# Transposed attention weights copied slot by slot, opening preparation in both banks of a slot, sums spread one period later

## The chip, the cores and the metric

The kernel runs on one core of a Trainium2 chip, in one launch. The metric is the device time of one execution in microseconds (us). Three timed executions of the kernel before took 701.68, 701.98 and 702.99 us; the median is 701.98 us.

## What is computed

The input is attention data q, k, v (2 batches, 8 heads, 1152 rows, 64 columns) and the weights of a small mixture of four experts. All numbers are fp32.

```
q_pool = q.reshape(B, H, S // 2, 2, D).mean(axis=3)      # 576 pooled rows per head
attn   = softmax(q_pool @ k.T / sqrt(D))                  # 576 x 1152 per head
x      = (attn @ v) laid out as 1152 rows x 512 columns
p      = domain_probs / domain_probs.sum(-1)
out    = sum over 4 experts of p[:, e] * (relu(x @ w1[e]) @ w2[e])
```

## The kernel before, in words

**Two stages.** The first 300 us or so are attention, the rest is the mixture of experts (MoE). Attention works on 8 pairs of heads, one after the other (pair 0 to pair 7). A pair has 9 tiles of 128 rows by 1152 columns, and the loop at the end of the attention stage takes one tile per turn. Such a turn is called a period here: period i (0 to 8) of a pair. In front of the loop stands the opening, which prepares pair 0 and computes the scores of the first two tiles.

**A period** issues, in this order: the transposes of tile g (`T_chunk`, twice), the exponentials of tile g+1 (`exps`, ACT), a part of the product with v (`PV_part`, PE), now and then a spread of the sums (`spread_sums`), one piece of preparation for the next pair (`prep_q` or `prep_k`), and the scores of tile g+2 (`scores`). Every engine runs its own instructions strictly in the order in which they are issued here; semaphores tie the engines together. No scheduler moves anything.

**Names in the rows.** `pt` are the transposes of the exponentials on PE: 18 of them, 10 in the first chunk and 8 in the second. `po` is the product with v on PE, with 256 columns (periods 4 to 8) or 320 columns (periods 0 to 3). `spt` is the score product on PE. `sx` on DVE (L254) scales the scores and takes their row minimum, and `sx` on ACT (L260) is the exponential. `aT` is the copy of transposed weights from PSUM. `pq` and `pk` are the transposes that prepare q and k of the next pair. Prepared values are kept as a high and a low part: ACT writes the high part, DVE subtracts it and writes the low part. `pr` is the spread of the reciprocal sums over the partitions (PE, of a diagonal matrix `dg` that POOL builds), `rb` its copy on ACT.

**PSUM.** The transposes, the preparation and the spreads share a pool `ps_t` of two slots. A slot has two banks of 512 words per partition. `T_chunk` fills both banks of a slot, one bank for each half `a` of the rows; everything else uses bank 0 only. The scores have one slot of three banks, so the scores of a tile start only when DVE has read those of the tile before. The pool hands out whichever slot is due by its own rule when the program is built, and it orders accesses: an instruction that touches a slot waits for those before it that touched the same tile, and a new tile in a slot waits for the last reader of the old one.

**The copies.** Each chunk of `T_chunk` has two copies, `for a in range(2)` at L275: half 0 by ACT (L285), half 1 by DVE (L283).

**The spread.** `diag_sums` builds `dg` on POOL at the end of periods 3 and 8; `SPREAD = {7: (0, 0), 0: (-1, 1)}` (L380) calls `spread_sums` in period 7 for the pair itself and in period 0 for the pair before. `finish` uses the result in periods 8 and 3.

Of the kernel before, what the change touches and what calls it, by code (L numbers as in the profile page):

```python
# [8 lines left out]
F32 = mybir.dt.float32  # L9
F32R = mybir.dt.float32r  # L10
AF = mybir.ActivationFunctionType
# [6 lines left out]
def attention_moe_kernel(ctx, tc, q, k, v, probs, w1, w2, out):  # L18
    nc = tc.nc
# [3 lines left out]
    P = 128  # L23
    HALF = 64
# [87 lines left out]
    with ExitStack() as actx:  # L112
        ap = actx.enter_context(tc.tile_pool(name="ap", bufs=1))
        ps_t = actx.enter_context(tc.tile_pool(name="ps_t", bufs=2, space=PSUM))
# [8 lines left out]
        aT = [ap.tile([P, 2, KT, w], F32, name=f"aT{i}") for i, w in enumerate(GW)]  # L123
# [28 lines left out]
        def add_q0(eng, t0, t1):  # L152
            eng.tensor_tensor(
                qs[:, t0:t1], qn[:, t0:t1, 0, :].unsqueeze(2).to_broadcast([P, t1 - t0, 2, D]),
                qn[:, t0:t1, 1, :].unsqueeze(2).to_broadcast([P, t1 - t0, 2, D]), ALU.add)
# [11 lines left out]
        def split_k0(h, t0, t1):  # L167
            hi, lo = khl[:, h, t0:t1, 0, :], khl[:, h, t0:t1, 1, :]
            nc.scalar.activation(hi, kn[:, h, t0:t1], AF.Copy)
            nc.vector.tensor_tensor(lo, kn[:, h, t0:t1], hi.bitcast(F32), ALU.subtract)  # L170
# [9 lines left out]
        def q_split(hi, lo, src):  # L180
            nc.scalar.activation(hi, src, AF.Copy)  # L181
            nc.vector.tensor_tensor(lo, src, hi.bitcast(F32), ALU.subtract)  # L182

        def prep_q(n, c):
            pt = ps_t.tile([P, 2, 512], F32, tag="t", name="pq")[:, 0].rearrange("p (a b) -> p a b", a=4)
            if c == 2:
                src = qs[:, 8].rearrange("p z d -> p (z d)") if n == 0 else qsum[:, 8:].rearrange("p t d -> p (t d)")
                nc.tensor.transpose(pt[:, 0, :], src, ident)
                d, rows = q2m[n % 2], [slice(0, HALF), slice(HALF, P)]
                for r in rows:  # L190
                    nc.scalar.activation(d[r, 0, r], pt[r, 0, r], AF.Copy)
                for r in rows:
                    nc.vector.tensor_tensor(d[r, 1, r], pt[r, 0, r], d[r, 0, r].bitcast(F32), ALU.subtract)
                return
            for i in range(4):
                src = qs[:, 4 * c + i].rearrange("p z d -> p (z d)") if n == 0 else (
                    qsum[:, 2 * i:2 * i + 2].rearrange("p t d -> p (t d)"))
                nc.tensor.transpose(pt[:, i, :], src, ident)
            src = pt.rearrange("p t (s x) -> p s t x", s=2)
            if n == 0:  # L200
                d = [q2[0][:, z, :, 256 * c:256 * c + 256].rearrange("p s (t x) -> p s t x", x=HALF) for z in range(2)]
                q_split(d[0], d[1], src)
                return
            q_split(stq[:, 0], stq[:, 1], src)
            for y in range(2):
                for half in range(2):
                    r = slice(half * HALF, (half + 1) * HALF)
                    dst = q2[n % 2].rearrange("p z s (y x) -> p (z s) y x", y=2)[r, :, y, :]
                    src = stq.rearrange("p z s j x -> p (z s) (j x)")[y * HALF:(y + 1) * HALF]
                    nc.sync.dma_start(dst.bitcast(F32), src.bitcast(F32))  # L210
# [6 lines left out]
        KCH = [(0, 4), (4, 8), (8, 12), (12, 16), (16, 18)]  # L217
        KCH0 = [(0, 4), (4, 8), (8, 9), (9, 13), (13, 17), (17, 18)]

        def prep_k(n, c):  # L220
            f0, f1 = KCH[c] if n else KCH0[c]
            pt = ps_t.tile([P, 2, 512], F32R, tag="t", name="pk")[:, 0].rearrange("p (a b) -> p a b", a=4)
            for i in range(f0, f1):
                nc.tensor.transpose(  # L224
                    pt[:, i - f0, :], khl[:, i // KT, i % KT].rearrange("p z d -> p (z d)"), identr)
            dst = k2[n % 2].rearrange("p h s -> p (h s)")[:, f0 * P:f1 * P]
            src = pt[:, :f1 - f0, :].bitcast(F32).rearrange("p a b -> p (a b)")
            if c in (1, 3):
                nc.vector.tensor_copy(dst, src)
            else:  # L230
                nc.scalar.activation(dst, src, AF.Copy)
# [26 lines left out]
        def exps(g):  # L258
            n, i = tiles[g]
            nc.scalar.activation(sx[g % 3], sx[g % 3], AF.Exp, bias=mn[g % 3], scale=-1.0,  # L260
                                 accum_out=sums[n % 2][:, i:i + 1])
# [4 lines left out]
        def T_chunk(g, c):  # L266
            n, i = tiles[g]
            k0, k1 = TCH[c]
            ks = slice(k0, k1)
            pt = ps_t.tile([P, 2, 512], F32, tag="t", name="pt")[:, :, :(k1 - k0) * HALF]  # L270
            pt = pt.rearrange("p a (k x) -> p a k x", x=HALF)
            for kt in range(k0, k1):
                for a, r in enumerate(ROWS):
                    nc.tensor.transpose(pt[:, a, kt - k0, :], sx[g % 3][r, kt * P:(kt + 1) * P], ident[r, r])  # L274
            for a in range(2):  # L275
                if i == 8:
                    dst = aT[1][:, a, ks, 256:320]
                else:
                    j, h = divmod(i, 2)
                    x0 = (j % 2) * P + a * HALF  # L280
                    dst = aT[j // 2][:, h, ks, x0:x0 + HALF]
                if a:
                    nc.vector.tensor_copy(dst, pt[:, a])  # L283
                else:
                    nc.scalar.activation(dst, pt[:, a], AF.Copy)  # L285

        opt = {}

# [28 lines left out]
        def spread_sums(n, grp):  # L317
            pt = ps_t.tile([P, 2, 512], F32, tag="t", name="pr")[:, 0]
            w = GW[grp]
            for h in range(2):  # L320
                nc.tensor.matmul(pt[h * HALF:(h + 1) * HALF, :w], ones, dg[:, h, :w], start=True, stop=True)  # L321
            nc.scalar.activation(rb[grp], pt[:, :w], AF.Copy)
# [17 lines left out]
        def scores(g):  # L340
            if g < NTL:
                for c in range(3):
                    S_chunk(g, c)
                neg_scores(g)
# [9 lines left out]
        add_q0(nc.vector, 0, 4)  # L354
        split_k0(0, 0, 4)
        split_k0(0, 4, 9)
        prep_q(0, 0)
        for c in range(3):
            prep_k(0, c)
        add_q0(nc.gpsimd, 4, 9)  # L360
        split_k0(1, 0, 9)
        scores(0)
        for c in range(3, 6):
            prep_k(0, c)
        exps(0)
        scores(1)
        prep_q(0, 1)
        prep_q(0, 2)
        load_q(1)
        load_kv(kn, k, 1)  # L370
# [6 lines left out]
        PVCUT = {0: (1, -1, 0, 3), 1: (1, -1, 3, 5), 2: (1, -1, 5, 7), 3: (1, -1, 7, 9),  # L377
                 4: (0, 0, 0, 2), 5: (0, 0, 2, 4), 6: (0, 0, 4, 6), 7: (0, 0, 6, 8), 8: (0, 0, 8, 9)}
        STAGES = {0: [(stack_k, 0, 0)], 1: [(stack_k, 0, 1)], 3: [(diag_sums, 0, 0)], 8: [(diag_sums, 0, 1)]}
        SPREAD = {7: (0, 0), 0: (-1, 1)}  # L380
        PREP = [None, ("q", 0), ("k", 0), ("k", 1), ("k", 2), ("q", 2), ("k", 3), ("k", 4), None]

        def pv_part(g):
            n, i = divmod(g, 9)
            grp, dn, k0, k1 = PVCUT[i]
            if 0 <= n + dn < NP:
                PV_part(n + dn, grp, k0, k1)
# [28 lines left out]
        for g in range(NTL):  # L416
            n, i = divmod(g, 9)
# [9 lines left out]
            for c in range(2):  # L427
                T_chunk(g, c)
            if g + 1 < NTL:
                exps(g + 1)  # L430
            pv_part(g)
            if i in SPREAD and n + SPREAD[i][0] >= 0:
                spread_sums(n + SPREAD[i][0], SPREAD[i][1])
            if n + 1 < NP:
                if PREP[i]:
                    kind, c = PREP[i]
                    (prep_q if kind == "q" else prep_k)(n + 1, c)
            elif i >= 7:
                fill(4)
# [117 lines left out]
```

## Time and profile before

| what | value |
|---|---|
| median of three timed runs | 701.98 us |
| profiled execution, its own time | 703.03 us |
| span of the profiled execution | 701.2 us |
| busy share: PE, weight loads, DVE, ACT, POOL | 95%, 79%, 38%, 33%, 29% |
| chain that ended last: PE, DVE, issue, POOL, ACT | 80%, 14%, 2%, 2%, 2% |
| attention loop, first to last tile | 16.6 to about 291 us |

The chain that ended last is followed back from the last instruction, at each step to what released it. In the MoE stage it stays on PE. In the attention stage it goes back and forth between PE and DVE, with POOL once per pair. Busy shares are means over two stages with different limits, so they say little about either; a pair of the attention stage is read from the timeline instead. A row of the timeline gives the start, the duration, engine and line, operation and names, and in brackets how long the engine was idle before it and what ended that.

### The profile page before, as it was taken

How to read it: one execution, taken by the hardware profiler on the slowest of the kernel's cores; microseconds unless marked ns; L12 is line 12 of the kernel's file. 1: busy time of each engine (PE TensorE's matmuls, PEld its weight loads, DVE VectorE, ACT ScalarE, POOL GpSimd, SP SyncE). 2: the span in 40 equal slices, each digit the busy share in tenths (PEclk: the TensorE clock that was granted, in tenths of full speed). 3: DMA queues.
4: the chain of work that ended last, by engine and by line, in shares of the span. 5: the costliest groups of instructions: out<-in, count | busy, mean ns of one | idle time of the engine just before them, and what ended most of it. 6: DMA issues, size and time to landing. Idle time of an engine off the chain costs nothing.

```text
span 701.2 us, 11265 instructions
## 1 busy us (share of the span) xinstructions
PE 667.6 (95%) x4634; PEld 551.5 (79%) x4634; DVE 267.4 (38%) x525; ACT 228.9 (33%) x474; POOL 201.5 (29%) x242
## 2 busy tenths in 40 slices
PE   7799999999898989899999999999999999999998
PEld 5666666666666666679898989999898989898987
DVE  5666666666666666422121212122122212121211
ACT  4666666666666666412020101011110101010200
POOL 4213232323232442467061052080080350120000
PEclk7999999999999999999999999999999999999999
DMA  6715353535353770114011011030020010001012
GB/s 221 179 36 125 105 129 104 128 103 131 100 125 106 168 207 3 62 42 139 1 61 60 1 55 65 1 100 20 1 91 31 17 44 1 0 1 31 15 37 56
DMA packets 26452, 50.84 MB, mean 73 GB/s; under 512 B 2464, under 2 KB 9888, under 8 KB 26400
## 3 DMA queue, kind: packets, MB, share of 16 engines
q1 hardware_dynamic: 26400, 50.12, 25.5%
q8 instruction: 37, 0.61, 0.3%
q14 instruction: 15, 0.12, 0.1%
HBM read 30.97 MB, written 2.36 MB: 48 GB/s over the span
## 4 chain that ended last, share of the span: by engine, by line
PE 80%; DVE 14%; issue 2%; POOL 2%; ACT 2%; ACTq 0%; POOLq 0%
PE p L505 28%; PE p L92 27%; PE spt L251 12%; DVE sx L254 10%; PE po L298 4%; PE pk L224 3%; PE pt L274 2%; PE p1t L92 2%; DVE aT L283 2%; PE pr L321 2%; POOL dg L310 1%; DVE q2all L182 1%; POOL dg L314 1%; ACT q2all L181 1%; PE warm L353 0%
## 5 line engine op out<-in xcount | busy, mean ns | idle before, releaser
L92 PE MATMUL p<-xh,wslot 128*128 128x384 f32 x640 | 166.8, 339 | 1.2 <-DVE q2all L95 1.2
L254 DVE TENSOR_SCALAR_CACHE_REDUCE sx<-spt 128x1152 f32<-128x1152 f32 x72 | 97.7, 1356 | 78.0 <-PE spt L251 77.8
L92 PEld LDWEIGHTS p<-xh,wslot 128*128 128x128 f32 x640 | 116.6, 188 | 1.9 <-DVE q2all L95 1.5
L92 PE MATMUL p<-xl,wslot 128*128 128x384 f32 x320 | 108.3, 338 | 0.0
L260 ACT ACTIVATE sx<-sx,mn 128x1152 f32<-128x1152 f32 x72 | 90.6, 1258 | 21.0 <-DVE sx L254 17.9
L251 PE MATMUL spt<-k,q2all 128*128 128x384 f32 x384 | 85.3, 357 | 1.5 <-DVE sx L254 1.2
L298 PE MATMUL po<-aT,vn 128*64 128x320 f32 (+1 forms) x576 | 85.0, 418 | 0.0
L94 ACT ACTIVATE hb<-p 128x384 fp32r<-128x384 f32 x48 | 23.6, 492 | 161.4 <-PE p L92 158.3
L505 PE MATMUL p<-wslot,hb 128*128 128x512 f32 (+1 forms) x348 | 75.8, 375 | 0.0
L285 ACT ACTIVATE aT<-pt 128x320 f32<-128x320 f32 (+1 forms) x144 | 53.0, 409 | 66.7 <-PE pt L274 65.1
L251 PEld LDWEIGHTS spt<-k,q2all 128*128 128x128 f32 x384 | 65.8, 193 | 10.8 <-DVE sx L254 4.8
L505 PEld LDWEIGHTS p<-wslot,hb 128*128 128x128 f32 x348 | 62.2, 188 | 11.7
L510 DVE SCALAR_TENSOR_TENSOR acc<-p,pw,acc 128x512 f32<-128x512 f32 (+1 forms) x28 | 20.5, 731 | 124.1 <-PE p L505 124.1
L274 PEld LDWEIGHTS pt<-ident,sx 64*128 64x128 f32 x1296 | 47.7, 140 | 24.7 <-issue 9.3
L274 PE MATMUL pt<-ident,sx 64*128 64x64 f32 x1296 | 59.4, 230 | 4.0 <-DVE q2all L182 1.2
L92 PEld LDWEIGHTS p<-xl,wslot 128*128 128x128 f32 x320 | 60.0, 188 | 0.4
L283 DVE COPY aT<-pt 128x320 f32<-128x320 f32 (+1 forms) x144 | 58.5, 447 | 1.6 <-ACT aT L285 1.6
L94 ACT ACTIVATE k<-p 128x384 fp32r<-128x384 f32 x30 | 14.8, 492 | 130.6 <-PE p L92 130.6
L338 POOL TENSOR_TENSOR xl<-xs,xh 128x256 fp32r<-128x256 f32 (+2 forms) x20 | 13.4, 677 | 150.9 <-ACT xh L337 150.9
L95 DVE SCALAR_TENSOR_TENSOR hb<-p,hb 128x384 fp32r<-128x384 f32 x48 | 26.8, 558 | 78.1 <-ACT hb L94 78.1
L98 POOL TENSOR_SCALAR wslot<-stg 128x512 fp32r<-128x512 f32 x12 | 7.5, 622 | 161.5 <-PE p L92 84.0
L505 PE MATMUL p<-wslot,k 128*128 128x512 f32 x168 | 51.9, 390 | 0.0
(103 smaller groups left out, 767.1 us busy)
## 6 DMA issues: line engine op xcount, KB each, us to landing
kab<-k SPq DMA_DIRECT2D x32, 288.0 KB, 4.2
q2all<-q2all SPq DMA_DIRECT2D x28, 256.0 KB, 4.9
vn<-in_v_dram SPq DMA_DIRECT2D x8, 576.0 KB, 7.5
kn<-in_moe_w_dram SPq DMA_DIRECT2D x8, 512.0 KB, 3.8
qn<-in_moe_w_dram SPq DMA_DIRECT2D x8, 512.0 KB, 3.8
stg<-in_moe_w_dram SPq DMA_DIRECT2D x8, 512.0 KB, 3.6
qs<-in_moe_w_dram SPq DMA_DIRECT2D x8, 512.0 KB, 3.8
qn<-in_q_dram SPq DMA_DIRECT2D x7, 576.0 KB, 6.5
```

What stands on the lines that cost most here:

```text
L92: nc.tensor.matmul(pt, w[:, a, kt, fs], x[:, kt, cols], start=(j == 0), stop=(j == last))
L94: nc.scalar.activation(hh[ft], pt, AF.Relu)
L95: nc.vector.scalar_tensor_tensor(hl[ft], pt, 0.0, hh[ft].bitcast(F32), ALU.max, ALU.subtract)
L224: nc.tensor.transpose(pt[:, i - f0, :], khl[:, i // KT, i % KT].rearrange("p z d -> p (z d)"), identr)
L251: nc.tensor.matmul(spt[g][:, c, :NC], w, x, start=(j == 0), stop=(j == len(ops) - 1))
L254: nc.vector.tensor_scalar(sx[g % 3].rearrange("p (c x) -> p c x", c=3), spt.pop(g)[:, :, :NC], -INV, None, ALU.mult, ALU.min, accum_out=mn ...
L260: nc.scalar.activation(sx[g % 3], sx[g % 3], AF.Exp, bias=mn[g % 3], scale=-1.0, accum_out=sums[n % 2][:, i:i + 1])
L274: nc.tensor.transpose(pt[:, a, kt - k0, :], sx[g % 3][r, kt * P:(kt + 1) * P], ident[r, r])
L283: nc.vector.tensor_copy(dst, pt[:, a])
L285: nc.scalar.activation(dst, pt[:, a], AF.Copy)
L298: nc.tensor.matmul(po[h * HALF:(h + 1) * HALF, :w], vn[n % 2][:, h, kt, :], aT[grp][:, h, kt, :], start=(kt == 0), stop=(kt == KT - 1))
L505: nc.tensor.matmul(pc, h[ft][:, ts_], where[e, 2, ft // 4][:, a, ft % 4, c0:c1], start=(m == 0), stop=(m == len(ops) - 1))
```

## The change

It has three parts.

**Copies.** `T_chunk` now copies a whole chunk with one instruction: both halves of chunk 0 by ACT, both halves of chunk 1 by DVE.

**Opening.** `prep_q` and `prep_k` may be given a bank. `prep_bank` takes a slot and hands out its two banks one after the other, as parts of one tile; the first eight preparations of the opening use it.

**Spread.** The second spread of a pair moves from period 0 to period 1 of the next pair.

```diff
--- before.py
+++ after.py
@@ -181,8 +181,18 @@
             nc.scalar.activation(hi, src, AF.Copy)
             nc.vector.tensor_tensor(lo, src, hi.bitcast(F32), ALU.subtract)
 
-        def prep_q(n, c):
-            pt = ps_t.tile([P, 2, 512], F32, tag="t", name="pq")[:, 0].rearrange("p (a b) -> p a b", a=4)
+        banks = []
+
+        def prep_bank(name):
+            if not banks:
+                t = ps_t.tile([P, 2, 512], F32, tag="t", name=name)
+                banks.extend([t[:, 0], t[:, 1]])
+            return banks.pop(0)
+
+        def prep_q(n, c, pt=None):
+            if pt is None:
+                pt = ps_t.tile([P, 2, 512], F32, tag="t", name="pq")[:, 0]
+            pt = pt.rearrange("p (a b) -> p a b", a=4)
             if c == 2:
                 src = qs[:, 8].rearrange("p z d -> p (z d)") if n == 0 else qsum[:, 8:].rearrange("p t d -> p (t d)")
                 nc.tensor.transpose(pt[:, 0, :], src, ident)
@@ -217,9 +227,11 @@
         KCH = [(0, 4), (4, 8), (8, 12), (12, 16), (16, 18)]
         KCH0 = [(0, 4), (4, 8), (8, 9), (9, 13), (13, 17), (17, 18)]
 
-        def prep_k(n, c):
+        def prep_k(n, c, pt=None):
             f0, f1 = KCH[c] if n else KCH0[c]
-            pt = ps_t.tile([P, 2, 512], F32R, tag="t", name="pk")[:, 0].rearrange("p (a b) -> p a b", a=4)
+            if pt is None:
+                pt = ps_t.tile([P, 2, 512], F32, tag="t", name="pk")[:, 0]
+            pt = pt.bitcast(F32R).rearrange("p (a b) -> p a b", a=4)
             for i in range(f0, f1):
                 nc.tensor.transpose(
                     pt[:, i - f0, :], khl[:, i // KT, i % KT].rearrange("p z d -> p (z d)"), identr)
@@ -272,17 +284,15 @@
             for kt in range(k0, k1):
                 for a, r in enumerate(ROWS):
                     nc.tensor.transpose(pt[:, a, kt - k0, :], sx[g % 3][r, kt * P:(kt + 1) * P], ident[r, r])
-            for a in range(2):
-                if i == 8:
-                    dst = aT[1][:, a, ks, 256:320]
-                else:
-                    j, h = divmod(i, 2)
-                    x0 = (j % 2) * P + a * HALF
-                    dst = aT[j // 2][:, h, ks, x0:x0 + HALF]
-                if a:
-                    nc.vector.tensor_copy(dst, pt[:, a])
-                else:
-                    nc.scalar.activation(dst, pt[:, a], AF.Copy)
+            if i == 8:
+                dst = aT[1][:, :, ks, 256:320]
+            else:
+                j, h = divmod(i, 2)
+                dst = aT[j // 2][:, h, ks, (j % 2) * P:(j % 2 + 1) * P].rearrange("p k (a x) -> p a k x", a=2)
+            if c:
+                nc.vector.tensor_copy(dst, pt)
+            else:
+                nc.scalar.activation(dst, pt, AF.Copy)
 
         opt = {}
 
@@ -354,17 +364,17 @@
         add_q0(nc.vector, 0, 4)
         split_k0(0, 0, 4)
         split_k0(0, 4, 9)
-        prep_q(0, 0)
+        prep_q(0, 0, prep_bank("pk0"))
         for c in range(3):
-            prep_k(0, c)
+            prep_k(0, c, prep_bank("pk0"))
         add_q0(nc.gpsimd, 4, 9)
         split_k0(1, 0, 9)
         scores(0)
         for c in range(3, 6):
-            prep_k(0, c)
+            prep_k(0, c, prep_bank("pk0"))
         exps(0)
         scores(1)
-        prep_q(0, 1)
+        prep_q(0, 1, prep_bank("pk0"))
         prep_q(0, 2)
         load_q(1)
         load_kv(kn, k, 1)
@@ -377,7 +387,7 @@
         PVCUT = {0: (1, -1, 0, 3), 1: (1, -1, 3, 5), 2: (1, -1, 5, 7), 3: (1, -1, 7, 9),
                  4: (0, 0, 0, 2), 5: (0, 0, 2, 4), 6: (0, 0, 4, 6), 7: (0, 0, 6, 8), 8: (0, 0, 8, 9)}
         STAGES = {0: [(stack_k, 0, 0)], 1: [(stack_k, 0, 1)], 3: [(diag_sums, 0, 0)], 8: [(diag_sums, 0, 1)]}
-        SPREAD = {7: (0, 0), 0: (-1, 1)}
+        SPREAD = {7: (0, 0), 1: (-1, 1)}
         PREP = [None, ("q", 0), ("k", 0), ("k", 1), ("k", 2), ("q", 2), ("k", 3), ("k", 4), None]
 
         def pv_part(g):
```

**Where instructions move: DVE in the loop.** The rows are DVE's, in periods 2 and 3 of pair 0, from one scaling of the scores (`sx`) to the next; what an instruction waits for stands in brackets. Before:

```order
L283 COPY aT0_97<-pt_308 128x5x64 [waits Activation_49]
L283 COPY aT0_97<-pt_321 128x4x64 [waits Activation_49]
L254 TENSOR_SCALAR sx1_95,mn1_107<-spt_339 128x1152 [waits DVE_49,PE_49]
L283 COPY aT0_97<-pt_347 128x5x64 [waits Activation_49]
L283 COPY aT0_97<-pt_360 128x4x64 [waits Activation_49]
L229 CAST k2_1_90<-pk_372 128x512 [waits PE_49]
L254 TENSOR_SCALAR sx2_96,mn2_108<-spt_378 128x1152 [waits DVE_49,PE_49]
```

And in the changed program, at the same place:

```order
L293 COPY aT0_97<-pt_312 128x2x4x64 [waits PE_49]
L266 TENSOR_SCALAR sx1_95,mn1_107<-spt_329 128x1152 [waits DVE_49,PE_49]
L293 COPY aT0_97<-pt_349 128x2x4x64 [waits PE_49]
L241 CAST k2_1_90<-pk_360 128x512 [waits PE_49]
L266 TENSOR_SCALAR sx2_96,mn2_108<-spt_366 128x1152 [waits DVE_49,PE_49]
```

DVE has one copy per period in place of two, of the second chunk only (`4x64` twice), and it waits for PE and no longer for ACT's copy of the other half. ACT loses the copy of the second chunk and gains the other half of the first.

**PE where one pair goes over into the next.** The rows are PE's in periods 0 and 1 of pair 1. Before:

```order
L274 MATMUL pt<-ident,sx_94 128x64 x18
L298 MATMUL po<-aT_98,vn_92 64x320 x6
L321 MATMUL pr<-dg,ones 64x320 x2
L251 MATMUL spt<-k_1_90,q2all 128x384 x6
L274 MATMUL pt<-ident,sx_95 128x64 x18
L298 MATMUL po<-aT_98,vn_92 64x320 x4
L198 MATMUL pq<-ident,qs 128x128 x4
```

Changed:

```order
L286 MATMUL pt<-ident,sx_94 128x64 x18
L308 MATMUL po<-aT_98,vn_92 64x320 x6
L263 MATMUL spt<-k_1_90,q2all 128x384 x6
L286 MATMUL pt<-ident,sx_95 128x64 x18
L308 MATMUL po<-aT_98,vn_92 64x320 x4
L331 MATMUL pr<-dg,ones 64x320 x2
L208 MATMUL pq<-ident,qs 128x128 x4
```

The spread `pr` now stands one period later, ahead of the transposes of q, and so ACT's copy `rb` stands ahead of its copy of `pq`. (A row's count is that of the program; the trace shows two passes for each `po` and `pr`.)

**PE and ACT in the opening.** The rows are PE's, from the first transposes of q (`qs`) to those of the second head of k. Before:

```order
L198 MATMUL pq_144<-ident_60,qs_72 128x128 x3
L224 MATMUL pk_151<-identr_76,khl_73 128x128 [waits DVE_49]
L224 MATMUL pk_157<-identr_76,khl_73 128x128 [waits DVE_49,Activation_49]
L224 MATMUL pk_163<-identr_76,khl_73 128x128 [waits DVE_49]
L251 MATMUL spt_169<-k2_0_74,q2all_75 128x384 x2
...
L224 MATMUL pk_177<-identr_76,khl_73 128x128 [waits DVE_49]
...
L224 MATMUL pk_183<-identr_76,khl_73 128x128 [waits PE_49]
```

Changed, where the two banks of a slot are one tile (`pk0_144`, `pk0_156`, `pk0_175`):

```order
L208 MATMUL pk0_144<-ident_60,qs_72 128x128 x3
L236 MATMUL pk0_144<-identr_76,khl_73 128x128 [waits DVE_49]
L236 MATMUL pk0_156<-identr_76,khl_73 128x128 [waits Activation_49]
L236 MATMUL pk0_156<-identr_76,khl_73 128x128 [waits DVE_49]
L263 MATMUL spt_167<-k2_0_74,q2all_75 128x384 [waits Activation_49]
...
L236 MATMUL pk0_175<-identr_76,khl_73 128x128 [waits DVE_49,PE_49]
...
L236 MATMUL pk0_175<-identr_76,khl_73 128x128 [waits DVE_49]
```

Counted by the values of the semaphores, the first wait on DVE was for the low part of k and is now for the low part of q, which DVE writes two instructions later. The second piece in `pk0_156` waits for DVE's copy of the first, and the second in `pk0_175` likewise. On ACT the second copy out of `pk0_144` waits for DVE too. Before, from the high part of q on:

```order
L181 ACTIVATE q2all_75<-pq_144 128x2x256 [waits PE_49]
L231 ACTIVATE k2_0_74<-pk_151 128x512 [waits PE_49]
L231 ACTIVATE k2_0_74<-pk_163 128x128 [waits PE_49]
L169 ACTIVATE khl_73<-kn_69 128x9x64 [waits DMAHW2_49]
L231 ACTIVATE k2_0_74<-pk_183 128x512 [waits PE_49]
```

Changed:

```order
L181 ACTIVATE q2all_75<-pk0_144 128x2x256 [waits PE_49]
L243 ACTIVATE k2_0_74<-pk0_144 128x512 [waits DVE_49,PE_49]
L243 ACTIVATE k2_0_74<-pk0_156 128x128 [waits PE_49]
L169 ACTIVATE khl_73<-kn_69 128x9x64 [waits DMAHW2_49]
L243 ACTIVATE k2_0_74<-pk0_175 128x512 [waits DVE_49,PE_49]
```

The order on ACT is the same, and two of its copies have a wait more. The high part of the second head of k (`khl`, L169) stays behind the copy out of `pk0_156`.

## Rows read from the trace of the kernel before

**Rows 1.** Sums of waits: engine, line, waited for: us, times, longest.

```profile
PEld pk L224 <- DVE aT L283: 17.8, 28, 1.3
PEld pr L321 <- POOL dg L314: 12.7, 8, 1.6
```

**Rows 2.** Timeline of pair 3: the transposes that begin periods 0 to 8.

```profile
154.50 0.77 PE L274 MATMUL pt<-ident,sx 64*128 64x64 f32 x18
...
160.01 0.78 PE L274 MATMUL pt<-ident,sx 64*128 64x64 f32 x18
...
163.60 1.06 PE L274 MATMUL pt<-ident,sx 64*128 64x64 f32 x18
...
167.51 0.78 PE L274 MATMUL pt<-ident,sx 64*128 64x64 f32 x18
...
171.03 0.78 PE L274 MATMUL pt<-ident,sx 64*128 64x64 f32 x18
...
174.84 0.77 PE L274 MATMUL pt<-ident,sx 64*128 64x64 f32 x18
...
178.71 0.35 PEld L274 LDWEIGHTS pt<-ident,sx 64*128 64x128 f32 x8 [0.22 <-PE pt L274]
...
182.56 0.78 PE L274 MATMUL pt<-ident,sx 64*128 64x64 f32 x18
...
186.57 0.78 PE L274 MATMUL pt<-ident,sx 64*128 64x64 f32 x18
```

**Rows 3.** The same timeline, inside period 4: scaling, the two halves' copies, preparation.

```profile
171.14 1.36 DVE L254 TENSOR_SCALAR_CACHE_REDUCE sx<-spt 128x1152 f32<-128x1152 f32 x1 [0.42 <-PE spt L251]
...
171.60 0.71 ACT L285 ACTIVATE aT<-pt 128x320 f32<-128x320 f32 x2 [0.81 <-PE pt L274]
...
172.72 0.79 DVE L283 COPY aT<-pt 128x320 f32<-128x320 f32 x2
...
173.23 0.54 PE L224 MATMUL pk<-identr,khl 128*128 128x128 f32 x4 [0.41 <-DVE aT L283]
```

**Rows 4.** The same timeline, inside period 0: the spread.

```profile
158.08 0.76 PE L321 MATMUL pr<-dg,ones 128*64 128x320 f32 x4 [1.04 <-POOL dg L314]
```

**Rows 5.** Chain that ended last, pair 7: start, us, engine, name.

```profile
270.32 1.25 PE spt L251 x6
271.56 0.71 PE pt L274 x17
272.27 1.23 PE po L298 x8
...
275.45 1.01 PE po L298 x8
```

**Rows 6.** Groups by line and shape: us in total, mean ns, idle before.

```profile
L260 ACT ACTIVATE sx<-sx,mn 128x1152 f32<-128x1152 f32 x72 | 90.6, 1258 | 21.0 <-DVE sx L254 17.9 <-DVE rs L307 2.3
...
L283 DVE COPY aT<-pt 128x320 f32<-128x320 f32 x72 | 34.5, 480 | 1.0 <-ACT aT L285 1.0
L285 ACT ACTIVATE aT<-pt 128x320 f32<-128x320 f32 x72 | 31.5, 438 | 64.3 <-PE pt L274 64.3
...
L285 ACT ACTIVATE aT<-pt 128x256 f32<-128x256 f32 x72 | 27.3, 379 | 2.3 <-PE pt L274 0.7
...
L322 ACT ACTIVATE rb<-pr 128x320 f32<-128x320 f32 x8 | 3.5, 439 | 13.2 <-PE pr L321 13.2
```

**Rows 7.** Timeline of the opening: k of pair 0, low parts, first transposes.

```profile
5.27 0.75 PE L224 MATMUL pk<-identr,khl 128*128 128x128 f32 x4
...
6.16 0.69 DVE L182 TENSOR_TENSOR q2all<-pq,q2all 128x512 fp32r<-128x512 f32 x1 [0.52 <-ACT q2all L181]
...
8.26 1.68 DVE L170 TENSOR_TENSOR khl<-kn,khl 128x576 fp32r<-128x576 f32 x1 [0.28 <-ACT khl L169]
...
16.62 1.23 PE L274 MATMUL pt<-ident,sx 64*128 64x64 f32 x18 [1.20 <-DVE q2all L182]
```

**Rows 8.** Stretch of the opening: busy us by engine, then the granted clock.

```profile
16.60:17.80 1.20, 1.18 (x19) 1.06 (x19) 0.31 (x2) 0.34 (x1) 1.20 (x2) 0.50 0.87 303
```

## Prediction

> **What bounds the kernel now.** I first read the chain that ended last: in the MoE stage it stays on PE, which nothing of the change touches; in the attention stage it goes from DVE to PE and back. So I asked the sums of waits what PE waits for there. Two entries belong to the lines of the diff [rows 1]: the weight loads of `pk` wait for DVE's copy `aT` (28 times, 17.8 us), and those of `pr` for POOL's `dg` (8 times, 12.7 us; PE's own idle time before them is about 1 us each [rows 4]). Then I read one steady pair in the timeline. From its transposes [rows 2] periods 0, 1 and 2 last 160.01 - 154.50 = 5.51, 3.59 and 3.91 us, period 3 lasts 3.52, period 4 3.81, periods 5 and 6 together 182.56 - 174.84 = 7.72, period 7 4.01.
>
> What a period costs when PE waits for nothing shows in pair 7, which prepares no next pair: there the chain stays on PE [rows 5]. Transposes 0.71, `po` 1.01 at 256 columns and 1.23 at 320, scores 1.25 us. Eight matmuls with 64 columns more cost 0.22, so a column costs 0.43 ns. A piece of `pk` costs 0.36: in period 4 it starts at 173.23 [rows 3], and the next transposes at 174.84, 1.61 later, of which 1.25 are scores. In the same way `pr` at 320 columns costs 160.01 - 158.08 - 1.25 = 0.68 [rows 2, 4].
>
> **The copies.** In period 4, `pk` needs the slot of the first chunk. ACT's half is copied from 171.60 on; DVE's half starts at 172.72 only, since DVE reads the scores from 171.14 to 172.50 [rows 3], and PE goes on at 173.23 when that copy (0.48 [rows 6]) has ended. In the changed program ACT alone frees that slot. Its copy starts 0.57 after the transposes (171.60 - 171.03) and takes two halves of 320: from 0.44 at 320 elements and 0.38 at 256 [rows 6], 0.92 ns per element, I take 0.73. The slot is free 1.30 after the transposes began; transposes and `po` end at 0.71 + 1.01 = 1.72. So `po` hides the copy with 0.4 to spare, and PE becomes the bound of the period. ACT's own next work, the exponential, cannot start before DVE's scaling has ended, 1.47 after the transposes, so it loses nothing either. DVE's single copy lies between one row of 0.48 and two; it stands behind the scaling and its slot is wanted only later in the period or by the next one. The two ends for ACT's copy: 0.44, as for one half, which changes nothing, and 1.26, as for the exponential of 1152 elements [rows 6], which would put the slot at 1.83 and the exponential 0.3 later; I keep 0.73, nearest to the copies' own rows.
>
> Period 2: 0.71 + 1.23 + 0.36 + 1.25 = 3.55, 0.36 less. Period 3 is at that value already (3.52). Period 4: 0.71 + 1.01 + 0.36 + 1.25 = 3.33, 0.48 less. In period 6 the second chunk waits for the low part of q prepared in period 5, and begins at 178.71 [rows 2], 3.87 after the start of period 5; that chain (scaling, exponential, two small copies, DVE) is not touched. From there 8 of 18 transposes 0.32, `po` 1.01, `pk` 0.36, nine score matmuls 1.75 (six take 1.25, of which 6 x 384 x 0.43 ns = 0.99 grow with the columns): 3.87 + 3.44 = 7.31 for both periods, 0.41 less. Period 7: 0.71 + 1.01 + `pr` at 256 columns 0.57 + half a `pk` 0.18 + 1.25 = 3.72, 0.29 less. Period 8 has no preparation and keeps its length. A steady pair gains 1.54, six of them (pairs 1 to 6) 9.2. Pair 7 has only period 7: 0.3. Pair 0 has no `po` in its first four periods, so its periods 1 to 3 were bound by the same wait with nothing else on PE; I take 2.0, between the steady 1.5 and 2.5. Copies together: -11.5.
>
> What is late next is PE itself, and in periods 1 and 5 the chain of q's preparation.
>
> The Trainium skill speaks for the old split: by Advanced Engine Details and Errata, section "Bank Collisions", ScalarE and VectorE read PSUM at the same time at full rate if they use different banks, so two halves on two engines should free a slot sooner than one engine with both. Here that is not so, because DVE's half starts 1.12 after ACT's [rows 3]. By the rule the sum would lose the -11.5; that is the second rival below.
>
> **The spread.** In period 0 PE stands still until POOL has built `dg`: `pr` starts at 158.08, 3.58 after the period's start, having waited 1.04 [rows 4]. Without it period 0 is 0.71 + 12 matmuls of `po` (1.23 x 12/8 less 0.07 for the fixed part) 1.78 + 1.25 = 3.74, 1.77 less. In period 1 `pr` comes some 5.7 after the same start, two microseconds after `dg`, so nothing waits; PE does 0.68 more there. Per pair -1.09, seven times (pairs 1 to 7): -7.6. ACT's `rb` (0.44 [rows 6]) now precedes the high part of q in period 1, and behind that stand DVE's low part and the scaling of the next scores. Since the period itself is 0.68 longer, this chain ends about where the scores do; I count it as hidden. Uncovered it would cost up to 0.44 a pair. POOL and SP keep their orders; the preparations of q come 0.7 later relative to their period, and what their DMAs bring is read six periods on.
>
> **The opening.** Two banks share a tile, and the program orders all that touches a tile. Before, k's first transposes run at 5.27 beside the split of q; now they wait for q's low part, which ends at 6.16 + 0.69 = 6.85 [rows 7]: 1.6 later. Its third piece waits for DVE's copy of the second, and on ACT the high part of the second head stands behind that third piece, so DVE's low part of it (8.26 [rows 7]) moves by about the same 1.6. From there the fifth piece waits for DVE's copy of the fourth, which stands behind the scaling of tile 0. I put the first transposes of the loop, 16.62, 2.2 later. Bounds: 0, if later steps have slack that the rows don't show, and 1.6 + two copies of about 0.7 + 0.7 more = 3.7. There the granted clock is 0.50 [rows 8], the 1.2 GHz level, and 18 transposes cost 1.23 instead of 0.78. It rises after PE has been busy for some time; a later dense stretch may mean one more stretch at 1.2 GHz, for which I add 0.3. Opening: +2.5.
>
> By the Trainium skill (PSUM — Partial Sum Buffer, "PSUM bank collisions raise a hardware error") accesses need guarding by bank, so two banks of a slot need no order. Were the program to follow that, the opening would not lose; that is the first rival.
>
> **The sum.** -11.5 - 7.6 + 2.5 = -16.6. The profiled execution took 703.03 (span 701.2 and 1.8 around it), 1.05 above the median of the timed runs. From its own time 686.4, from the median 685.4; I say 686.0.
>
> **Rivals.** *The opening is free or gains*: the extra bank outweighs the order. For it: PE waits in the opening for copies of `k`; against it: the waits in the program. -19 or a little more, 683.
>
> *The copies give nothing*: the slot is late in another way, by ACT behind its exponentials, so that only spread and opening count: 702.0 - 7.6 + 2.5 = 696.9. For it: ACT gets the bigger share (640 of 1152 elements); against it: its idle time before `aT`, 0.81 in [rows 3].
>
> *The q chain of period 1 becomes the bound*: 7 x 0.44 = 3.1 more, 689.1. For it: every step of that chain waits for the one before; against it: the 0.68 that PE takes at the same place.
>
> *Slower*: ACT's copy over two banks is far slower than by its rows and holds up the exponential, and so the next transposes. A period is then 0.57 + copy + 1.36 (the exponential and the gap before it) and more; it passes the old 3.81 from a copy of about 1.9 on. At 2.2 it costs 0.3 in each of 64 periods, 19 us, and with the other terms 702 + 19 - 7.6 + 2.5 = 716. No row comes near: the exponential reads more elements in 1.26.
>
> **Chances.** My forecast 0.64 (684 to 688.5), opening free 0.09, q chain 0.13, copies give nothing or half 0.09, slower 0.03; 0.02 for no change at all. Range 682 to 691.5. A difference under 0.2% (1.4 us) can't be told from none here: faster 0.95, same 0.02, slower 0.03.
>
> **What would show it.** Right: no wait of `pk` for `aT` on DVE in periods 2 to 7 but in q's periods; period 0 at 3.7 and period 1 at 4.3; a steady pair 2.6 shorter; ACT's copy at 0.7 to 0.75; the loop's first transposes near 18.8. Wrong: a copy over 1 us, a steady pair less than 1 shorter, an idle PE before `pr` in period 1, or a loop that begins at or before 16.6.

## The result and the profile after

The changed kernel takes 683.8 us (median of 4 runs, 683.43 to 684.12) where the kernel before takes 702.49 in the same comparison. The ratio is 0.9734, with a 95% interval of 0.9717 to 0.9751. The forecast was 686.0, 2.2 us more than that. The profiled execution took 684.09 (span 682.3); against 703.03 that is 18.9 less.

Busy times and the chain that ended last come first. The share of the chain on DVE falls from 14% to 4%, that on PE rises from 80% to 90%.

```profile
PE 663.2 (97%) x4634; PEld 553.6 (81%) x4634; DVE 257.9 (38%) x453; ACT 226.1 (33%) x402; POOL 201.4 (30%) x242
PE 90%; DVE 4%; ACT 4%; issue 1%; POOL 0%; ACTq 0%; POOLq 0%
```

Next the sums of waits (who waits <- for whom: us, times, longest). They answer to [rows 1]: `pk` waits for DVE's `aT` 7 times instead of 28, all of them in period 7, where `pk` comes behind `pr`; `pr` waits for `dg` once, in the last pair, instead of 8 times. The transposes that wait for the low part of q (third line) are the second chunk of period 6. That wait is older than the change: in the kernel before, this chunk began at 178.71 [rows 2], 0.12 after the low part had ended, and the profile put the wait down to PE.

```profile
PEld pk L236 <- ACT aT L295: 3.2, 8, 0.5
PEld pk L236 <- DVE aT L293: 2.7, 7, 0.4
PE pt L286 <- DVE q2all L203: 2.4, 7, 0.4
PEld pr L331 <- POOL dg L324: 1.6, 1, 1.6
```

The two new copies, from the costliest groups (busy, mean ns | idle before). By [rows 6], 0.73 us were forecast for ACT's.

```profile
L295 ACT ACTIVATE aT<-pt 128x640 f32<-128x640 f32 x72 | 50.7, 705 | 55.9 <-PE pt L286 55.8
L293 DVE COPY aT<-pt 128x512 f32<-128x512 f32 x72 | 49.0, 680 | 1.5 <-PE pt L286 1.5
```

Pair 4 in the timeline answers to [rows 2]: start, duration, and the idle time before it where there is one. Counted from pair 0, the rows that [rows 2] calls pair 3 are those of pair 4 too; pairs 1 to 6 are so alike that nothing else changes by it.

```profile
145.57 0.77 PE L286 MATMUL pt<-ident,sx 64*128 64x64 f32 x18
149.29 0.78 PE L286 MATMUL pt<-ident,sx 64*128 64x64 f32 x18
153.42 0.87 PE L286 MATMUL pt<-ident,sx 64*128 64x64 f32 x18
157.06 0.78 PE L286 MATMUL pt<-ident,sx 64*128 64x64 f32 x18
160.58 0.78 PE L286 MATMUL pt<-ident,sx 64*128 64x64 f32 x18
163.88 0.78 PE L286 MATMUL pt<-ident,sx 64*128 64x64 f32 x18
...
167.78 0.46 PE L286 MATMUL pt<-ident,sx 64*128 64x64 f32 x8 [0.33 <-DVE q2all L203]
171.29 0.78 PE L286 MATMUL pt<-ident,sx 64*128 64x64 f32 x18
...
177.83 0.77 PE L286 MATMUL pt<-ident,sx 64*128 64x64 f32 x18
```

The pair lasts 177.83 - 145.57 = 32.26 us where it lasted 35.04. Inside period 4, which answers to [rows 3], DVE's copy still starts as late as before (1.68 after the transposes), but `pk` goes on 0.04 after that copy *started*: it follows ACT's copy, which ended at 161.84, and PE's own `po`.

```profile
160.68 1.36 DVE L266 TENSOR_SCALAR_CACHE_REDUCE sx<-spt 128x1152 f32<-128x1152 f32 x1 [0.42 <-PE spt L263]
161.14 0.70 ACT L295 ACTIVATE aT<-pt 128x640 f32<-128x640 f32 x1 [0.81 <-PE pt L286]
162.26 0.66 DVE L293 COPY aT<-pt 128x512 f32<-128x512 f32 x1
162.30 0.54 PE L236 MATMUL pk<-identr,khl 128*128 128x128 f32 x4
```

The opening answers to [rows 7, 8]. k's first transposes stand at 6.72, released by q's low part, and the loop begins at 18.19 instead of 16.62. The last line is the window from 18 to 20 (busy and count of the five engines, then the granted clock): it is still 0.50 there.

```profile
6.72 0.88 PE L236 MATMUL pk<-identr,khl 128*128 128x128 f32 x8 [1.41 <-DVE q2all L182]
9.65 0.76 DVE L170 TENSOR_TENSOR khl<-kn,khl 128x576 fp32r<-128x576 f32 x1 [1.31 <-ACT khl L169]
18.19 1.22 PE L286 MATMUL pt<-ident,sx 64*128 64x64 f32 x18 [1.20 <-DVE q2all L182]
18.00:20.00 2.00, 1.81 (x20) 1.70 (x21) 1.02 (x4) 0.97 (x2) 1.92 (x3) 0.50 0.71 272
```

Where the 18.9 us of the two profiled executions went, from such starts: the opening +1.57; pair 0 (loop's begin to pair 1's begin) 32.76 to 30.37, -2.39; pairs 1 to 6 210.26 to 193.75, -16.51; pair 7, up to its last transposes, -1.6; all that follows +0.05.

### The profile page after: what moved, and what is told of

Same layout as the page of the kernel before. It is cut to its first block, busy times and chain, and to the rows that moved or that the text cites. A ratio compares the mean times of both kernels' runs of the same rounds, so it can differ in the third digit from the quotient of the medians.

```text
span 682.3 us, 11118 instructions
## 1 busy us (share of the span) xinstructions
PE 663.2 (97%) x4634; PEld 553.6 (81%) x4634; DVE 257.9 (38%) x453; ACT 226.1 (33%) x402; POOL 201.4 (30%) x242
## 4 chain that ended last, share of the span: by engine, by line
PE 90%; DVE 4%; ACT 4%; issue 1%; POOL 0%; ACTq 0%; POOLq 0%
PE p L515 29%; PE p L92 27%; PE spt L263 10%; PE po L308 10%; PE pt L286 6%; ACT sx L272 3%; DVE sx L266 3%; PE pk L236 2%; PE p1t L92 2%; PE pr L331 1%; PE pq L208 1%; PE warm L363 0%; DVE q2all L203 0%; ACT q2all L201 0%; ACT q2all L181 0%
## 5 line engine op out<-in xcount | busy, mean ns | idle before, releaser
L295 ACT ACTIVATE aT<-pt 128x640 f32<-128x640 f32 x72 | 50.7, 705 | 55.9 <-PE pt L286 55.8
L308 PEld LDWEIGHTS po<-aT,vn 128*64 128x64 f32 x576 | 35.3, 136 | 20.3
```

Source lines behind the costliest of these rows:

```text
L295: nc.scalar.activation(dst, pt, AF.Copy)
L308: nc.tensor.matmul(po[h * HALF:(h + 1) * HALF, :w], vn[n % 2][:, h, kt, :], aT[grp][:, h, kt, :], start=(kt == 0), stop=(kt == KT - 1))
```

## The experiments

**One part at a time.** The first three kernels are the kernel before with one part each: the copies, the line `SPREAD`, the banks of the opening. The fourth is the changed kernel without its opening part (the pieces of q and k take bank 0 of a slot each, as before). The kernel before took 702.38 beside them.

```diff
-            for a in range(2):
...
-                if a:
-                    nc.vector.tensor_copy(dst, pt[:, a])
-                else:
-                    nc.scalar.activation(dst, pt[:, a], AF.Copy)
+            if c:
+                nc.vector.tensor_copy(dst, pt)
+            else:
+                nc.scalar.activation(dst, pt, AF.Copy)
```

> The kernel before with the merged copies of T_chunk alone; sums still spread in period 0, opening as before. Theory (ACT alone frees the first slot early, and PE becomes the bound of the period): steady periods 2, 4, 5 and 6, 7 lose 0.3 to 0.5 us each, pair 0 loses 2.4, together some 11.5 us, about 691. Period 0 keeps its 5.5 us and its wait for POOL's dg. Rival (the copies give little by themselves and the gain is the spread's): 697 or more.

Measured: 690.86, ratio 0.9839 (0.9819 to 0.9858).

```diff
-        SPREAD = {7: (0, 0), 0: (-1, 1)}
+        SPREAD = {7: (0, 0), 1: (-1, 1)}
```

> The kernel before with the sums of group 1 spread in period 1 instead of 0, nothing else. Theory (period 0 loses its wait for dg and the 0.68 us of pr, period 1 takes pr without a wait): 7 pairs times 1.1 to 1.25, 7.6 to 8.8 us less, 694 to 695. Rival (with the old copies, pr in period 1 is one more user of the two slots and waits for DVE's half copy as pk does, some 0.4 more in each pair): 5 us less, about 697.5, and a period 1 of 4.6 us or more.

Measured: 694.13, ratio 0.9885 (0.9866 to 0.9904).

```diff
-        prep_q(0, 0)
+        prep_q(0, 0, prep_bank("pk0"))
         for c in range(3):
-            prep_k(0, c)
+            prep_k(0, c, prep_bank("pk0"))
...
```

> The kernel before with the opening's preparation in both banks of a slot, nothing else. Theory (two banks of one tile are ordered as one tile, so k's first transposes wait for q's low part): loop begins at 18.2 instead of 16.6, the time is 1.6 us longer, about 704.1. Rival 1 (the opening's loss is given back in pair 0, where something else is late): 702.5. Rival 2 (the longer stretch at the lower granted clock costs more on top): 705 or more.

Measured: 704.49, ratio 1.0034 (1.0022 to 1.0046); the loop begins at 18.27.

The changed kernel without those lines:

```diff
-        prep_q(0, 0, prep_bank("pk0"))
+        prep_q(0, 0)
...
```

> The changed kernel without its opening part: merged copies and the spread in period 1, opening as before. Theory (the three parts add up): 1.6 us less than the changed kernel, about 682.2, loop begins at 16.6. Rival (the opening's loss is hidden or given back): 683.8, as the changed kernel.

Measured: 681.56, ratio 0.9704 (0.9685 to 0.9723); the loop begins at 16.39.

So the copies give 11.5, the spread 8.3, and the opening takes 2.1; together that would be -17.7, and the change gave -18.7. Each of these times is uncertain by a good 1 us, so the missing 1.0 alone would say nothing. The period lengths of pair 4 show which part acts where, and that there is an interaction:

| period | before | copies alone | spread alone | changed |
|---|---|---|---|---|
| 0 | 5.51 | 5.52 | 3.71 | 3.72 |
| 1 | 3.59 | 3.58 | 4.36 | 4.13 |
| 2 | 3.91 | 3.80 | 3.75 | 3.64 |
| 3 | 3.52 | 3.52 | 3.52 | 3.52 |
| 4 | 3.81 | 3.31 | 3.79 | 3.30 |
| 5 and 6 | 7.72 | 7.41 | 7.71 | 7.41 |
| 7 | 4.01 | 3.56 | 4.02 | 3.57 |
| 8 | 2.97 | 2.97 | 2.97 | 2.97 |

With the old copies the moved `pr` costs period 1 0.77; with the new ones 0.54. Here the rival of the second run was half right: a third user of the two slots loses time to DVE's half copy too, 0.23 a pair, and the new copies take that away as well. In the run with the spread alone, the first of DVE's two half copies ends at 155.74 + 0.48 = 156.22 and `pr` starts 0.15 later, 1.31 after `po` (1.12 in the changed kernel):

```profile
155.74 0.82 DVE L283 COPY aT<-pt 128x320 f32<-128x320 f32 x2
...
156.37 0.76 PE L321 MATMUL pr<-dg,ones 128*64 128x320 f32 x4
```

That `pr` waits for that copy is read from this distance; the profile names no wait of PE there.

Period 2 shortens by 0.11 with the copies alone and by 0.16 with the spread alone. In the kernel before, its second chunk of transposes waits until DVE has read `pq` for q's low part, and no copy of `aT` has a hand in that:

```profile
164.19 0.33 PEld L274 LDWEIGHTS pt<-ident,sx 64*128 64x128 f32 x8 [0.21 <-DVE q2all L182]
```

With `pr` in period 1 the low part ends 4.49 after that period's begin instead of 4.12 (changed kernel and copies alone), but the period itself is 0.55 longer, so most of this wait goes.

**Is it the engine that frees a slot, or that four copies became two?** First the engines of the two copies were exchanged:

```diff
-            if c:
+            if not c:
                 nc.vector.tensor_copy(dst, pt)
```

> The changed kernel with the engines of the two merged copies exchanged: first slot by DVE, second by ACT. Theory (what counts is that the engine that is free first frees the slot that is wanted first): DVE's copy starts behind the scaling, 1.7 us after the transposes, and takes 0.8, so the slot is free at 2.5 where PE wants it at 1.7 to 1.9; the waits of pk for DVE's copy come back and are longer than before, and the copies' 11.5 us are lost with some us more, 695 to 702. Rival (the gain is that four copies became two): 684 to 686.

Measured: 685.53, ratio 0.9763 (0.9746 to 0.9779). My expectation missed by 9.5 us or more, and the rival's number came true. Period 4 of that kernel shows why:

```profile
162.51 0.60 ACT L295 ACTIVATE aT<-pt 128x512 f32<-128x512 f32 x1 [1.05 <-PE pt L286]
...
163.38 0.79 DVE L293 COPY aT<-pt 128x640 f32<-128x640 f32 x1
163.41 0.54 PE L236 MATMUL pk<-identr,khl 128*128 128x128 f32 x4
```

`pk` again starts as soon as DVE's copy has *begun*, behind ACT's. In that kernel ACT copies the second chunk only, and 21 of the waits of `pk` are for ACT's copy:

```profile
PEld pk L236 <- ACT aT L295: 9.2, 21, 0.8
```

So it was given the slot of the second chunk there, where in period 4 of the changed kernel it has that of the first: the slots are not dealt out in a fixed turn. It looks as though the one that is expected to come free first is taken; no run tests that rule. The exchange therefore didn't test what I meant it to. Where `pr` takes that slot and `pk` gets the other, in period 7, the kernel is 0.11 longer in each pair (3.68 against 3.57). The next run separates the two causes: four copies again, but both halves of a slot by one engine.

```diff
+            for a in range(2):
...
-            if c:
-                nc.vector.tensor_copy(dst, pt)
-            else:
-                nc.scalar.activation(dst, pt, AF.Copy)
+                if c:
+                    nc.vector.tensor_copy(dst, pt[:, a])
+                else:
+                    nc.scalar.activation(dst, pt[:, a], AF.Copy)
```

> The changed kernel with each slot's copy made in two halves again, as before the change, but both halves of a slot by the same engine: the first slot by ACT, the second by DVE. Theory (what counts is that one of the two slots comes free by ACT alone, whatever number of copies that takes; two halves of 320 took ACT 0.71 in the kernel before, as long as one of 640): as the changed kernel, 683.5 to 685.5. Rival (the gain is that four copies became two): the copies' 11.5 us are lost, 694 to 696.

Measured: 683.92, ratio 0.9742 (0.9721 to 0.9763), the time of the changed kernel. Its 144 copies on ACT keep it busy for 55.1 us, 0.77 for the two of a slot (they overlap a little), where one merged copy is 0.705; the 0.71 of the expectation was the row of one half of 320 and one of 256. `pk` waits for ACT's copy no longer than in the changed kernel (3.3 us in 8 waits, there 3.2 in 8):

```profile
L297 ACT ACTIVATE aT<-pt 128x320 f32<-128x320 f32 x144 | 55.1, 435 | 56.2 <-PE pt L286 56.1
PEld pk L236 <- ACT aT L297: 3.3, 8, 0.6
```

So the number of copies is not the cause. What counts is that one slot comes free without DVE. How much a `pk` that had only DVE's slot in periods 4 and 6 would lose, no run shows.

**How much cover is left for ACT's copy?** ACT makes it twice:

```diff
                 nc.scalar.activation(dst, pt, AF.Copy)
+                nc.scalar.activation(dst, pt, AF.Copy)
```

> The changed kernel in which ACT makes its copy of the first slot twice, to the same place (0.70 us more on ACT in each of 72 tiles). Theory (the rest of a period's transposes and po hide a copy that ends by 1.72 us after the transposes began, 0.4 to 0.5 after the present end): the slot is free at 2.0, PE waits about 0.3 in periods 4 to 7 and little in 2 and 3, 1 to 1.3 us a pair, 691 to 694. Rival 1 (copies are hidden altogether): 684. Rival 2 (ACT's exponential sets the next transposes, so that all of the 0.70 shows in each period): 684 + 72 x 0.7 = 734.

Measured: 701.09, ratio 0.9985 (0.9976 to 0.9995): 17.3 us more than the changed kernel, above the theory and below rival 2. In periods 4 to 7 the theory held: they are 1.21 us longer in pair 4. What it left out are periods 1 and 8, longer by 0.31 and 0.32. Period 8 has no `pk` at all and still goes from 2.97 to 3.30 (here in pair 6):

```profile
254.88 0.78 PE L286 MATMUL pt<-ident,sx 64*128 64x64 f32 x18
255.45 0.70 ACT L295 ACTIVATE aT<-pt 128x640 f32<-128x640 f32 x1 [0.88 <-PE pt L286]
256.18 0.71 ACT L296 ACTIVATE aT<-pt 128x640 f32<-128x640 f32 x1
256.78 1.25 ACT L272 ACTIVATE sx<-sx,mn 128x1152 f32<-128x1152 f32 x1
258.18 0.77 PE L286 MATMUL pt<-ident,sx 64*128 64x64 f32 x18 [0.43 <-ACT sx L272]
```

The exponential starts 1.90 after the transposes instead of 1.57, and the next transposes wait for it. Of the extra 0.70, 0.33 shows there and 0.37 was hidden, most of it in ACT's idle time of 0.29 ahead of its exponential. The forecast's 0.4 to spare was that of the slot; the nearer limit is the exponential. In the changed kernel's period 8 these rows stand so (the 0.29 is the cover):

```profile
174.86 0.78 PE L286 MATMUL pt<-ident,sx 64*128 64x64 f32 x18
175.43 0.70 ACT L295 ACTIVATE aT<-pt 128x640 f32<-128x640 f32 x1 [0.67 <-PE pt L286]
176.43 1.26 ACT L272 ACTIVATE sx<-sx,mn 128x1152 f32<-128x1152 f32 x1 [0.29 <-DVE sx L266]
```

**Does q's chain bind period 1?** The spread was moved one period further.

```diff
-        SPREAD = {7: (0, 0), 1: (-1, 1)}
+        SPREAD = {7: (0, 0), 2: (-1, 1)}
```

> The changed kernel with the sums of group 1 spread in period 2 instead of 1. Theory (period 1 is PE's own work, no chain of q's preparation binds it): period 1 goes from 4.13 to about 3.6, period 2 from 3.63 to about 4.2, and the time stays at 684 within 1. Rival (in period 1 the copy of the sums on ACT holds up q's preparation and with it the next scores): 0.44 less in each of 7 pairs, about 681.

Measured: 684.7, ratio 0.9756 (0.9739 to 0.9773). Pair 4's starts give 3.59 for period 1 and 4.33 for period 2:

```profile
148.97 0.78 PE L286 MATMUL pt<-ident,sx 64*128 64x64 f32 x18
152.56 0.52 PE L286 MATMUL pt<-ident,sx 64*128 64x64 f32 x10
...
156.89 0.78 PE L286 MATMUL pt<-ident,sx 64*128 64x64 f32 x18
```

The 0.54 that period 1 gives up come back as 0.69 in period 2: the rival falls. Seven pairs by 0.15 would be 1.05; the medians differ by 0.9, which the intervals can't tell from none.

**The opening.** Two kernels start from the one without the opening part. In the first, DVE makes POOL's addition of q's second part, later, at a place where DVE is idle:

```diff
-        add_q0(nc.gpsimd, 4, 9)
         split_k0(1, 0, 9)
         scores(0)
         for c in range(3, 6):
             prep_k(0, c)
+        add_q0(nc.vector, 4, 9)
```

> The kernel without the opening part (merged copies, spread in period 1), in which the opening's addition of q's second part is made by DVE, at a place where DVE is idle, instead of POOL. Theory (DVE's low part of k's second head takes 1.7 instead of 0.76 us where POOL's addition runs at the same time, and PE, which waits for it, falls to the lower granted clock): the low part takes 0.76, PE waits less, the granted clock stays at 1.00 for longer, loop begins at 14.2 to 15 instead of 16.4, time 679.5 to 680.5. Rival (the 1.7 us come from something else, such as the loads still arriving): low part still 1.7, time as without the opening part, 681.6.

Measured: 680.61, ratio 0.9697 (0.9682 to 0.9713). The low part takes 0.76, as expected; the loop begins at 15.79, later than expected, since the granted clock falls to 0.50 at about 8 us all the same. Against the kernel without the opening part (0.9704) the gain is inside the intervals. In the second, the opening's pieces have four tiles of one bank each:

```diff
+        first = ExitStack()
+        ps_1 = first.enter_context(tc.tile_pool(name="ps_1", bufs=4, space=PSUM))
...
+            pt = (ps_1.tile([P, 512], F32R, tag="t1", name="pk") if n == 0 else
+                  ps_t.tile([P, 2, 512], F32R, tag="t", name="pk")[:, 0]).rearrange("p (a b) -> p a b", a=4)
...
         prep_q(0, 2)
+        first.close()
+        ps_t = actx.enter_context(tc.tile_pool(name="ps_t", bufs=2, space=PSUM))
```

> The kernel without the opening part (merged copies, spread in period 1), in which the opening's pieces of q and k have four tiles of one bank each in place of two slots of two banks. Theory (the opening part lost time since two banks of one tile are ordered as one; with a tile for each bank nothing is ordered that needn't be): k's second piece no longer waits for ACT's copy, and the loop begins 0.5 to 2 us sooner than without the opening part, 679.5 to 681. Rival (more banks give nothing, since the copies and DVE's chain set the opening): 681.6. Rival (engines that use neighbouring banks hold each other up): 682 or more.

Measured: 678.6, ratio 0.9665 (0.9649 to 0.9682), the fastest version beside the next. Nine transposes of k run together from 5.26, released by nothing but their data, while ACT and DVE read q's bank beside them (5.52 to 6.84); the loop begins at 14.62; and the granted clock stays at 1.00 (window from 10 to 12), where it was 0.50 from about 10 to 20 without the opening part:

```profile
5.26 1.39 PE L227 MATMUL pk<-identr,khl 128*128 128x128 f32 x9
10.00:12.00 2.00, 1.22 (x7) 1.19 (x8) 0.72 (x3) 1.88 (x4) 0.00 (x0) 1.00 0.99 380
```

So two things changed at once, the order and the clock, and the run doesn't separate them. The old opening was as quick where the clock stayed at 1.00: in the profiled run with the copies alone, which has it, the loop begins at 14.14:

```profile
14.14 0.92 PE L274 MATMUL pt<-ident,sx 64*128 64x64 f32 x18 [1.52 <-DVE q2all L182]
```

Against that run the tiles of one bank gain nothing up to the loop's begin. That they make the clock stay high more often is possible and not shown.

Both together:

> The fastest so far (merged copies, spread in period 1, an opening with a tile for each bank) with the opening's addition of q's second part on DVE instead of POOL. Theory (DVE's low part waits for POOL's addition where they meet, 1.27 instead of 0.76 us): low part 0.76, loop begins some 0.5 sooner, at about 14.1, time 678.1. Rival (the addition's 0.8 us on DVE hold up the scaling of the next scores as much): 678.6 or a little more.

Measured: 678.57, ratio 0.9668 (0.965 to 0.9686). The loop begins at 14.07, as the theory says, but the time is the same: the expected 0.5 is within what the intervals can tell, and in its profile pair 0 lasts 0.67 longer than in the run before it (29.86 against 29.19). In this profile the granted clock falls to 0.50 inside pair 0, from 15.0 to 18.4, where it stays at 1.00 in the other:

```profile
16.00:18.00 2.00, 2.00 (x21) 1.42 (x20) 1.08 (x1) 0.97 (x3) 1.92 (x4) 0.50 0.84 240
```

## Why the prediction was right, point by point

**Copies, -11.5.** The mechanism is shown, by the run with the copies alone and by the one with four copies; 11.5 is what they gave alone (10.0 to 12.7 by the interval). That it fits to a tenth is luck, since its parts moved both ways. ACT's copy took 0.705 (0.73 forecast); periods 4, and 5 and 6, came out at 3.30 and 7.41 (3.33 and 7.31), period 7 at 3.57 (3.72). A steady pair gains 1.37 by the copies alone (33.67 against 35.04), not 1.54; pair 0 gave 2.39 in the changed kernel where 2.0 were taken. Period 2 was read wrongly: the prediction put all of its 0.36 down to the copies, and they alone give 0.11; it was q's low part that held its second chunk, the chain that the prediction named for periods 1 and 5 only. It came out at 3.64 (3.55 forecast) mostly by the spread. One sign did not come true as it was put: `pk` still waits for DVE's copy in period 7, 7 times and 2.7 us of weight loads, but PE shows no idle time at them. That ACT loses nothing held only just: some 0.3 is left, not 0.4, and by the exponential, not by the slot. The old split lost because DVE's half started 1.12 later [rows 3], whatever rate the two engines read at; so the rule by which the prediction weighed it (the Trainium skill, Advanced Engine Details and Errata, section "Bank Collisions") didn't decide, and the rival that rested on it fell.

**Spread, -7.6.** The mechanism was right, the size short: 8.3 alone (6.7 to 9.4), and 9.3 on top of the copies (690.86 to 681.56). Period 0 lasts 3.72 (3.74 forecast). Two things were left out: the 0.16 by which period 2 shortens, and a part of what `pr` costs. `pr` costs period 1 0.54, not 0.68, since `po` hands over to it after 1.12, not 1.23 [rows 5], and `pr` itself takes 0.64 up to the next piece, as pair 4's period 1 shows:

```profile
150.00 1.30 PE L308 MATMUL po<-aT,vn 128*64 128x320 f32 x8
...
151.12 0.71 PE L331 MATMUL pr<-dg,ones 128*64 128x320 f32 x4
...
151.76 0.66 PE L208 MATMUL pq<-ident,qs 128*128 128x128 f32 x4
```

Over seven pairs the cheaper `pr` is 1.0 us. The profiled executions differ from the sum by 2.3: 0.9 in the opening, 0.7 in pairs 1 to 6, 0.4 in pair 0 and 0.2 in pair 7. `rb` and q's chain stayed hidden.

**Opening, +2.5.** The part alone cost 2.1 (1.5 to 3.2), so the size is not refuted; the way to it was partly wrong. Up to the loop's begin the profiled executions differ by 1.57, not 2.2. The first steps came as forecast (k's transposes at 6.72, 1.45 later). But DVE's low part of the second head, which [rows 7] shows with 1.68, now takes 0.76, and so ends 0.47 later instead of 1.6 (10.41 against 9.94); the wait for the fourth piece's copy then added the rest. The 1.68 contained a wait for POOL that I had taken for work. The stretch at 0.50 lasts until 22, not 19.6; in both kernels it ends after PE had been busy without a gap (18 to 20 before, 20 to 22 changed). That is the kind of loss for which the forecast added 0.3; no run shows its price alone.

**The rivals.** "The opening is free" falls by the third run. Its mechanism, guarding by bank, was available all the same: in the kernel with a tile for each bank PE writes k's banks from 5.26 on while ACT and DVE read q's, which agrees with the Trainium skill's rule (PSUM — Partial Sum Buffer, "PSUM bank collisions raise a hardware error"). A tile of two banks was ordered by more than banks need: in the changed kernel the same transposes wait until 6.72. The 3 us by which that kernel is faster than the one without the opening part (678.6 and 681.56) are order and clock together. "The copies give nothing" and "slower" fall by the first run, "q's chain binds period 1" by the tenth.

## What to carry to other kernels

When two engines share one buffer's release, the later one sets it: give each buffer to one engine. The number of copies made no difference here (683.92 against 683.8), and which engine got which slot little (685.53), since the slot that ACT freed went to `pk` either way. Make a tile no larger than what must be ordered together, or the parts of it that have nothing to do with one another wait for each other. When a cover is estimated, take the nearest of all limits: here the slot had 0.4 to spare, the exponential on the same engine 0.3.

## What the runs showed that I had not expected

**DVE and POOL hold each other up.** The same DVE instruction, two SBUF inputs of 128x576, takes 0.76 alone. In the kernel before, POOL's addition was running when it began:

```profile
7.78 1.55 POOL L153 TENSOR_TENSOR qs<-qn 128x640 f32<-128x640 f32 x1 [5.55 <-DMA qn<-in_q_dram]
```

It ends at 9.33, and DVE's low part [rows 7] at 9.94, 0.61 behind it. In the kernel with a tile for each bank POOL ends at 8.23 and DVE at 8.84, again 0.61 behind:

```profile
6.67 1.56 POOL L154 TENSOR_TENSOR qs<-qn 128x640 f32<-128x640 f32 x1 [4.44 <-DMA qn<-in_q_dram]
7.57 1.27 DVE L171 TENSOR_TENSOR khl<-kn,khl 128x576 fp32r<-128x576 f32 x1
```

In the run with the copies alone DVE was first, and POOL's addition took 1.91 instead of 1.55:

```profile
7.98 0.76 DVE L170 TENSOR_TENSOR khl<-kn,khl 128x576 fp32r<-128x576 f32 x1 [0.31 <-ACT khl L169]
8.24 1.91 POOL L153 TENSOR_TENSOR qs<-qn 128x640 f32<-128x640 f32 x1 [6.01 <-DMA qn<-in_q_dram]
```

DVE ends at 8.74 there, and POOL at 10.15, 1.41 behind it. So the later one does most of its work after the earlier one has ended: 0.61 of 0.76, and 1.41 of 1.55. The Trainium skill says that a VectorE instruction with two SBUF inputs contends with a GpSimd instruction that reads SBUF (SBUF — State Buffer, "Who interferes with whom"); the rows agree, in both directions.

**The granted clock of the opening is not the same in every execution of one program text.** In the profiled run with the copies alone, whose opening is that of the kernel before, DVE came first at POOL's addition, the clock stayed at 1.00 until 15 us, and the loop began at 14.14, 2.5 us sooner than in [rows 7]. That this one meeting decides the clock is not shown: without POOL's addition (the kernel in which DVE makes it) the clock fell too. So a single profile of an opening is a poor measure of it: on record, thirteen executions of the kernel before, timed together, have mean granted clocks from 0.992 to 1.000.
